# Retention, then a token and channel mixer: later channel weights, both ch1 halves ahead of ch2, and u of batch 1 turned by the crossbar

## The chip, the cores and the metric

The kernel runs on one core of a Trainium2 chip. The metric is device time in microseconds (us): the median of the runs, 207.27 us before the change. Lower is better.

## The reference

For each batch and head a state decays and collects outer products of k and v; the output of a position is q times the state, scaled. The heads' outputs, side by side, are x. Two token matmuls mix x over the sequence, and two channel matmuls mix over the channels, both with a residual.

```python
B, H, S, D = 4, 8, 768, 64          # q, k, v: [B, H, S, D] float32
gamma = 1.0 - 2.0 ** (-5.0 - arange(H)); scale = 1 / sqrt(D)
for t in range(S):
    state = gamma * state + einsum('bhd,bhe->bhde', k[:, :, t], v[:, :, t])
    y[:, :, t] = scale * einsum('bhd,bhde->bhe', q[:, :, t], state)
x  = y.transpose(0, 2, 1, 3).reshape(B, S, H * D)               # 768 x 512 per batch
h  = maximum(x.T @ w_tok1, 0) @ w_tok2                          # 768 x 256, 256 x 768
u  = x + h.T
out = u + maximum(u @ w_ch1, 0) @ w_ch2                         # 512 x 1536, 1536 x 512
```

## The kernel before

The sequence is cut into six chunks of 128 positions, the eight heads into four pairs (p = 0 to 3). The work of a batch b has two parts.

**front(b, p)**, one per pair. `load` (L256, L252) brings the rows of q, k and v of two heads, 384 KB each in float32; batch 0 uses casting transfers of the POOL queue instead (L279, L282). k is scaled on DVE (L313), q and v are cast on POOL (L292). k and q are turned so that the head's dimension lies on the partitions: by TensorE transposes (L328, L332) and a copy (L340) in batches 0 and 1, by the DMA crossbar (`crossbar`, L347, on the SP queue) from batch XK = XQ = 2 on. L361 makes the chunks' outer products, L370 and L373 run them into states on DVE, L380 and L387 put these into r16. L403 makes the scores of a half (three chunks), L416 masks them, L437 and L440 make y, L451 and L455 scale it into x, and L468 casts x on POOL. Then come the token matmuls L491, L499 (relu) and L512, the residual L519 and a cast u on POOL (L530). u is turned as well: by three L543 transposes a half and a copy L552 for batches below XU = 2, else by one crossbar transfer a pair (L566, tile u16w, two buffers).

**back(b)**, the channel mixer, in two halves of 384 positions. ch1 makes 12 tiles with 4 matmuls each (L597) and a relu (L610) into a tile h2 (two buffers); ch2 makes 3 output tiles of 12 matmuls each (L626), a residual (L635) and a store (L642). Before the change a half does ch1 and then ch2, and then the next half does the same.

**The order.** A schedule is written out by the program itself. Every step is an `Op` with an engine, a priority, an occupation, a latency, what it depends on, and the buffers that it takes (`Slot`, counts in BUFS). `arrange` lists the Ops by a planned time: it keeps one free time for each engine and one for each transfer ring (SP and POOL), lets two rings share, and picks the next Op by priority among those that can start. The order it finds is what each engine issues; each engine works through its own list strictly in turn, so a step whose input is late holds up all that stand behind it on its engine. Before batch 0's mixer starts, L194 fills PE's planned gaps with matmuls on zeros.

**Weights.** `weight` issues wt1, wt2, two pieces of the ch1 weights (512 and 1024 KB in float16) and the ch2 weights (1536 KB) on the POOL queue with a cast (L203). All rows of batch 1 wait for the second ch1 piece; the wait is added by hand:

```python
if b == 1:
    tc.add_manual_dep(dma.ins, wops["c1", 1].ins.ins.name, ...,
                      reason="the weights come first")
```

The ch2 weights stand right behind it on the same queue, with no wait of their own.

Of the kernel before, what the change touches and what calls it, by code (L numbers as in the profile page):

```python
# [17 lines left out]
def kernel(  # L18
# [11 lines left out]
    nc = tc.nc  # L30
    B, H, S, D = q.shape
    P = 128
# [62 lines left out]
                x=3, uT=3, h2=2, o=3, r16=NR, fa=5, ba=3)  # L95
    SEM, GUARD = 80, 100
    EARLY, LATE, DIRECT = 1000, 12, 3
    LONG, XK, XQ, XU, XBAR = 2, 2, 2, 2, 1500
    RING = dict(SP=3, POOL=8)
    QLONG = 1200  # L100
    ASIDE, RACT = ((1, 1), (1, 3), (2, 1), (2, 3), (3, 1), (3, 3)), ()
    KPOOL = ()
    FILL, TOKBA = 0.75, 2
    ops = []

    class Slot:
# [15 lines left out]
    def arrange():  # L122


        way = {}
        for op in reversed(ops):
            if op.first is not None:
                way[op] = way.get(op, 0) + op.lat + SEM
                for d in op.deps:
                    way[d] = max(way.get(d, 0), way[op])  # L130
        for op in ops:
            if op.first is not None:
                op.prio = (op.prio[0], 0, EARLY * op.first - way[op], op.first)
        free = dict(PE=5700, ACT=5000, DVE=4600, POOL=1100, SP=1300, SPring=1300, POOLring=1300)
        taken = {t: [] for t in BUFS}
        todo, order, ring = list(ops), [], dict(SP=[], POOL=[])
        while todo:
            best = []
            for op in todo:
                if any(d.end is None for d in op.deps):  # L140
                    continue
                start = free[op.eng]
                if op.dma and len(ring[op.eng]) >= RING[op.eng]:
                    start = max(start, ring[op.eng][-RING[op.eng]])
                for d in op.deps:
                    if d.eng == op.eng and (d.dma or d.eng == "PE"):
                        continue
                    start = max(start, d.end + (30 if d.eng == op.eng else SEM) + op.guard)
                more = {}
                for s in op.takes:  # L150
                    q = taken[s.tag]
                    n = len(q) + more.get(s.tag, 0) - BUFS[s.tag]
                    more[s.tag] = more.get(s.tag, 0) + 1
                    if n >= 0:
                        old = q[n]
                        if any(u.end is None for u in old.users):
                            break
                        start = max([start] + [u.end + SEM for u in old.users])
                else:
                    best.append((start, op))  # L160
            t = min(b[0] for b in best)

            eng = min(best, key=lambda b: (b[0], b[1].prio))[1].eng
            start, op = min((b for b in best if b[1].eng == eng and b[0] <= t + 20),
                            key=lambda b: b[1].prio)
            free[op.eng] = start + op.occ
            op.start = start
            if op.dma:

                mine, other = op.eng + "ring", ("POOL" if op.eng == "SP" else "SP") + "ring"  # L170
                at = max(free[mine], start + (op.occ + 200 if op.eng == "POOL" else 50))
                both = max(0, free[other] - at)
                shared = min(op.dma, both // 2)
                free[mine] = at + op.dma + shared
                free[other] += shared
                op.end = free[mine] + 1600
                ring[op.eng].append(free[mine])
            else:
                op.end = start + op.lat
            for s in op.takes:  # L180
                taken[s.tag].append(s)
            todo.remove(op)
            order.append(op)
        return order
# [14 lines left out]
    wops = {}  # L199

    def weight(key, ns, out, src):
        def emit():
            return nc.gpsimd.dma_start(out=out, in_=src.rearrange("(i p) j -> p i j", p=P))  # L203
        wops[key] = Op("POOL", (0,) if key[0] != "c2" else (2, 0, 0), 800, 800, emit, dma=ns)

    weight(("t1", 0), 2000, wt1, moe_w_tok1)
# [3 lines left out]
    weight(("c2", 0), 7800, wc2, moe_w_ch2)  # L210


    queue, sp_done = [], [None]
    x_add, uT_done, y_done, t1_done, t2_done = {}, {}, {}, {}, {}
    xs, uTs = {}, {}
    rcount = [0]
# [1 line left out]
    def front(b, p):  # L218
        first = b == 0
# [23 lines left out]
        def load(nm):  # L243
            src, slot = srcs[nm]

            def emit():
                t = tile_of(slot, sb, [P, 2 * NC, D], FP)
                rows = src[b, 2 * p:2 * p + 2]
                eng = nc.gpsimd if first and p else nc.sync
                if nm == "q" and b < LONG:  # L250

                    dma = eng.dma_start(  # L252
                        out=t.rearrange("p (h f i) d -> p h f (i d)", h=2, f=2),
                        in_=rows.rearrange("h (f p i) d -> p h f (i d)", f=2, p=P))
                else:
                    dma = eng.dma_start(out=t, in_=rows.rearrange("h (c p) d -> p (h c) d", p=P))  # L256
                if b == 1:
                    tc.add_manual_dep(
                        dma.ins, wops["c1", 1].ins.ins.name,
                        mybir.DependencyInfo(mybir.DependencyClass.Sync, mybir.DependencyReason.DATA),  # L260
                        reason="the weights come first")
                return dma
            ns = QLONG if nm == "q" and b < LONG else 1750
            if first and p:
                o = Op("POOL", (0,), 1000, 1000, emit, [], [slot], dma=ns)
                queue.append(o)
            else:
                o = Op("SP", (0, b, p), 100, 100, emit,
                       deps=[sp_done[-1]] + ([wops["c1", 1]] if b == 1 else []), takes=[slot], dma=ns)
                sp_done.append(o)  # L270
            return o

        def cast(slot, nm):
# [24 lines left out]
        if first and p == 1:  # L298
            queue.append(Op("POOL", (0,), 520, 520, lambda: nc.gpsimd.affine_select(
                out=mask, in_=mask, compare_op=ALU.is_ge, fill=0.0,  # L300
# [43 lines left out]
        def crossbar(src, dst, dep):  # L344
            def emit():
                d = tile_of(dst, sb, [P, S], F16)
                return nc.sync.dma_start_transpose(  # L347
                    out=d.rearrange("d (c t) -> d c t", t=P),
                    in_=src.tile.rearrange("p c h d -> p (c h d)" if src is K else "p c d -> p (c d)"))
            return Op("SP", (-1, b, p), 100, 100, emit, [dep], [dst], [src], dma=XBAR)  # L350
        kt = crossbar(K, KT, kc) if b >= XK else turn(K, KT, kc, "DVE" if first else "ACT")
        qt = crossbar(Q, QT, qc) if b >= XQ else turn(Q, QT, qc, "ACT")

# [73 lines left out]
        for hf in range(2):  # L427
# [41 lines left out]
            tk = [X] if p == 0 and hf == 0 else []  # L469
# [31 lines left out]
        tt, uc = [], None  # L501
        wide = b >= XU
        T, UW = Slot(FA), Slot("u16w")
        for hf in range(2):
# [27 lines left out]
            uc = op("POOL", 450, 510, emit, [ad, uc] if wide else [ad], [U16] if new else [], [X] if new else [X, U16])  # L532
# [14 lines left out]
            if first or hf == 1:  # L547
                def emit(hf=hf, T=T):
                    if UT.tile is None:
# [3 lines left out]
                tk = [UT] if (b, "uT") not in uT_done else []  # L553
                dep = [] if tk else [uT_done[b, "uT"]]
                e = op("ACT", 380 if first else 700, 480 if first else 800, emit, [tt[-1]] + dep, tk,
                       [T] if tk else [T, UT])
# [5 lines left out]
        if wide:  # L562
            def emit():
                if UT.tile is None:
                    tile_of(UT, sb, [P, NP, S], F16)
                return nc.sync.dma_start_transpose(  # L566
                    out=UT.tile[:, p].rearrange("d (c t) -> d c t", t=P),
                    in_=UW.tile.rearrange("p c d -> p (c d)"))
            tk = [UT] if (b, "uT") not in uT_done else []
            e = Op("SP", (-1, b, p), 100, 100, emit, [uc] + ([] if tk else [uT_done[b, "uT"]]), tk,  # L570
                   [UW] if tk else [UW, UT], dma=XBAR)
            if tk:
                uT_done[b, "uT"] = e
            for s in range(2):
                uT_done[b, p, s] = e
# [3 lines left out]
    def back(b):  # L579
# [3 lines left out]
        def op(eng, occ, lat, emit, deps=(), takes=(), uses=()):  # L583
            seq[0] += 1
            return Op(eng, ((1 if eng == "PE" else 0), b, seq[0]), occ, lat, emit, deps, takes, uses)
        for sh in range(2):
            H2 = Slot("h2")
            rel = []
            for ft in range(NF):
# [17 lines left out]
                def emit(ft=ft, A=A, H2=H2):  # L607
                    if ft == 0:
                        tile_of(H2, sb, [P, NF, SH], F16)
                    nc.scalar.activation(H2.tile[:, ft], A.tile[:, :SH], AF.Relu)  # L610
                rel.append(op("ACT", 400, 490, emit, [c1] + rel[:1], [H2] if ft == 0 else [],
                              [A] if ft == 0 else [A, H2]))
            for i in range(HC):

                parts = 2 if (b, sh, i) == (B - 1, 1, HC - 1) else 1
                CW = C // parts
                for part in range(parts):
# [25 lines left out]
                    st = op("SP", 100, 100, emit, [ad], [], [O])  # L643
                    st.prio, st.dma = (-2, b), 800 // parts


    after = {(3, "v"): (("t1", 0), ("t2", 0))}
    for p in range(NP):
# [2 lines left out]
    for b in range(1, B):  # L651
        for p in range(NP):
            front(b, p)
    for one, two in zip(queue, queue[1:]):
        two.deps.append(one)
    for b in range(B):
        back(b)
# [39 lines left out]
```

## Time and profile before

| | |
|---|---|
| runs (us) | 207.62, 207.40, 205.96, 207.27, 205.78; median 207.27 |
| profiled execution | 205.29, of which the span is 203.6 |
| granted TensorE clock | 1.0 |
| busy, share of the span | PE 95%, DVE 55%, ACT 48%, POOL 34% |
| L597 (ch1) | 384 matmuls, 68.2 us busy |
| L626 (ch2) | 300 matmuls, 68.9 us busy |
| L194 (on zeros) | 37 in the larger group, 12.0 us |
| DMA | 32.55 MB, mean 160 GB/s; q1 (SP) 25.57 MB, q0 (POOL) 6.69 MB |
| ch2 weights, issue to landing | 23.4 us |
| k rows on SP, issue to landing | median 6.4 us |

How to read it: times count from the start of the span. PE is TensorE's matmuls, PEld its weight loads, which overlap them; matmuls are pipelined, so a busy PE may hold short gaps that show only between the starts of instructions. "<-" names what an instruction waited for.

### The profile page before, as it was taken

The numbers are of one execution on the slowest core, as the hardware profiler recorded it, in microseconds if no ns is written. First come the engines' busy times: TensorE is split into PE (matmuls) and PEld (weight loads), VectorE is DVE, ScalarE is ACT, GpSimd is POOL, SyncE is SP. The second block draws the span as 40 slices with busy tenths as digits, with TensorE's granted clock in tenths as the row PEclk, the third lists the DMA queues.
The fourth block names the chain that finished last, engine by engine and source line by source line (L and its number), as shares of the span: only waits on it lengthen the run. The fifth ranks groups of instructions, "written<-read, shape, count | busy, mean of one in ns | idle before, by whom it ended". The sixth has DMA issues, their size and how long they took to land.

```text
span 203.6 us, 4737 instructions
## 1 busy us (share of the span) xinstructions
PE 194.2 (95%) x1900; PEld 119.8 (59%) x1900; DVE 111.9 (55%) x285; ACT 97.3 (48%) x211; POOL 69.4 (34%) x116
## 2 busy tenths in 40 slices
PE   7898999779999999999999999999999999999993
PEld 2554796444587766676646656566657545545552
DVE  7399863017798889897296546947682021021021
ACT  7256797651499642465404650275115604604700
POOL 7998283033155643453442144125132000000000
PEclk9999999999999999999999999999999999999999
DMA  6999999999899989998998999898531112012012
GB/s 113 175 218 186 208 210 207 245 235 262 188 272 202 187 160 234 240 215 137 202 238 185 144 228 226 157 214 125 126 92 55 39 52 103 3 52 103 0 55 103
DMA packets 88470, 32.55 MB, mean 160 GB/s; under 512 B 79328, under 2 KB 84704, under 8 KB 88448
## 3 DMA queue, kind: packets, MB, share of 16 engines
q1 hardware_dynamic: 76128, 25.57, 61.8%
q0 software_dynamic: 12320, 6.69, 23.2%
q8 instruction: 15, 0.25, 0.5%
q14 instruction: 7, 0.06, 0.1%
HBM read 26.74 MB, written 6.29 MB: 162 GB/s over the span
## 4 chain that ended last, share of the span: by engine, by line
PE 78%; DMA 13%; POOL 6%; issue 1%; DVE 1%; POOLq 0%; SPq 0%
PE ba L626 31%; PE ba L597 28%; DMA wc<-in_moe_w_ch_dram 8%; DMA kf<-in_k_dram 5%; PE fa L512 4%; PE fa L491 4%; PE fa L403 3%; PE fa L440 2%; POOL v L282 2%; PE fa L437 2%; PE fa L361 2%; POOL kf L256 2%; PE fa L332 1%; POOL q L279 1%; POOL wt L203 1%
## 5 line engine op out<-in xcount | busy, mean ns | idle before, releaser
L626 PE MATMUL ba<-wc,h 128*128 128x512 f16 (+1 forms) x300 | 68.9, 371 | 0.0
L597 PE MATMUL ba<-uT,wc 128*128 128x384 f16 x384 | 68.2, 326 | 0.0
L610 ACT ACTIVATE h<-ba 128x384 f16<-128x384 f32 x96 | 46.4, 492 | 39.2 <-PE ba L597 38.7
L597 PEld LDWEIGHTS <-wc 128*128 128x128 f16 x384 | 36.0, 98 | 22.5
L626 PEld LDWEIGHTS <-h 128*128 128x128 f16 x300 | 27.2, 98 | 25.6
L635 DVE TENSOR_TENSOR o<-x,ba 128x512 f32<-128x512 f32 (+1 forms) x25 | 16.6, 662 | 42.2 <-PE ba L626 42.1
L416 DVE TENSOR_TENSOR am<-fa,mask 128x384 f16<-128x384 f32 x58 | 29.8, 549 | 11.8 <-PE fa L403 11.7
L468 POOL CAST x<-x 128x384 f16<-128x384 f32 x30 | 15.2, 516 | 29.2 <-issue 13.8
L519 DVE TENSOR_TENSOR x<-x,fa 128x384 f32<-128x384 f32 x28 | 14.5, 550 | 11.6 <-PE fa L512 11.2
L313 DVE TENSOR_SCALAR k<-kf,gk 128x384 f16<-128x384 f32 x32 | 15.1, 512 | 7.9 <-DMA kf<-in_k_dram 7.9
L451 ACT ACTIVATE x<-fa,gy 128x192 f32<-128x192 f32 (+1 forms) x42 | 14.9, 422 | 8.6 <-PE fa L440 8.6
L373 DVE SCALAR_TENSOR_TENSOR U<-U,gp,fa 128x64 f32<-128x64 f32 x64 | 17.4, 275 | 1.1
L292 POOL CAST q<-qf 128x768 f16<-128x768 f32 x12 | 10.2, 850 | 22.4 <-DMA qf<-in_q_dram 21.2
L380 ACT ACTIVATE r<-U 64x320 f16<-64x320 f32 x16 | 7.5, 467 | 20.1 <-DVE U L373 20.1
L530 POOL CAST u16w<-x 128x384 f16<-128x384 f32 x16 | 7.9, 509 | 20.3 <-DVE x L519 20.3
L194 PE MATMUL fa<-zero 128*128 128x512 f16 x37 | 12.0, 462 | 2.2 <-DVE zero L52 1.3
L440 PE MATMUL fa<-v,am 128*128 128x64 f16 x192 | 13.6, 193 | 0.0
L440 PEld LDWEIGHTS <-am 128*128 128x128 f16 x192 | 12.1, 98 | 2.3
L491 PEld LDWEIGHTS <-wt 128*128 128x128 f16 x192 | 11.9, 98 | 2.1
L512 PEld LDWEIGHTS <-wt 128*128 128x128 f16 x192 | 11.8, 98 | 2.2
L340 ACT COPY qT<-fa 128x768 f16<-128x768 f16 x8 | 11.6, 1449 | 2.8 <-PE fa L328 2.4
L292 POOL CAST v<-vf 128x768 f16<-128x768 f32 x12 | 10.0, 830 | 6.8 <-DMA vf<-in_v_dram 6.8
(60 smaller groups left out, 176.5 us busy)
## 6 DMA issues: line engine op xcount, KB each, us to landing
out_dram<-o SPq DMA_DIRECT2D x23, 256.0 KB, 2.4
kf<-in_k_dram SPq DMA_DIRECT2D x13, 384.0 KB, 6.4
qf<-in_q_dram SPq DMA_DIRECT2D x12, 384.0 KB, 5.9
vf<-in_v_dram SPq DMA_DIRECT2D x12, 384.0 KB, 5.3
wc<-in_moe_w_ch_dram POOLq DMA_DIRECT2D x1, 1536.0 KB, 23.4
kf<-in_k_dram POOLq DMA_DIRECT2D x3, 384.0 KB, 6.7
wc<-in_moe_w_ch_dram POOLq DMA_DIRECT2D x1, 1024.0 KB, 16.0
q<-in_q_dram POOLq DMA_DIRECT2D x4, 192.0 KB, 6.1
```

The lines of the kernel that those rows point to most:

```text
L292: nc.gpsimd.tensor_copy(t, src.tile.rearrange("p (h c) d -> p h c d", h=2))
L313: (nc.gpsimd if keng == "POOL" else nc.vector).tensor_scalar(k16[:, :, j, :], src, gk[:, h:h + 1], None, ALU.mult)
L373: nc.vector.scalar_tensor_tensor(U[:, c], U[:, c - 1], gp[:, p:p + 1], o, ALU.mult, ALU.add)
L416: nc.vector.tensor_tensor(am, src[:, :HC], mask, ALU.mult)
L440: nc.tensor.matmul(o[:, j * D:(j + 1) * D], AM[2 * hf + j].tile[:, i], V.tile[:, j * NC + c], start=(c == 0), stop=(c == 0 or j == 1))
L468: nc.gpsimd.tensor_copy(X16.tile[:, half(hf)], X.tile[:, half(hf), pc])
L491: nc.tensor.matmul(acc[:, jt * P:(jt + 1) * P], wt1[:, i, jt * P:(jt + 1) * P], X16.tile[:, i], start=(i == 0), stop=(i == NC - 1))
L512: nc.tensor.matmul(acc[:, i * P:(i + 1) * P], wt2[:, jt, t], H1.tile[:, jt], start=(jt == 0), stop=(jt == NJ - 1))
L597: nc.tensor.matmul(acc[:, :SH], w[:, ct, f * P:(f + 1) * P], UT.tile[:, ct, sh * SH:(sh + 1) * SH], start=(ct == 0), stop=(ct == NP - 1))
L610: nc.scalar.activation(H2.tile[:, ft], A.tile[:, :SH], AF.Relu)
L626: nc.tensor.matmul(A.tile[:, :CW], H2.tile[:, ft, i * P:(i + 1) * P], wc2[:, ft, cs], start=(ft == 0), stop=(ft == NF - 1))
L635: nc.vector.tensor_tensor(o[:, :CW], X.tile[:, sh * HC + i, cs], A.tile[:, :CW], ALU.add)
```

## The change

Four things are changed.

1. The issue of the ch2 weights waits for the v rows of batch 1's pair 1 (PRE = 2 pairs). The dependency enters the plan, and `weight` adds it by hand to the transfer. With it the issue moves on POOL behind batch 0's last casts and the first four casts of batch 1.
2. `back` is cut into `ch1(half)` and `ch2(half)`. For batch 0 (b < TWICE = 1) both halves of ch1 come before both halves of ch2; from batch 1 on the order stays.
3. XU goes from 2 to 1: u of batch 1 is turned by the crossbar (four transfers L566 on SP) and not by 24 transposes L543 and four copies L552.
4. The planner's numbers change: a crossbar transfer occupies SP for 1220 ns (100 before) and its ring for 1200 (1500 before), and a transfer of SP that is planned after 5 us starts only when POOL's ring is free. These change the order that comes out, on every engine.

```diff
-    LONG, XK, XQ, XU, XBAR = 2, 2, 2, 2, 1500
+    LONG, XK, XQ, XU, XBAR = 2, 2, 2, 1, 1200
...
-    FILL, TOKBA = 0.75, 2
+    FILL, TOKBA, PRE, TWICE = 0.75, 2, 2, 1
...
                 both = max(0, free[other] - at)
                 shared = min(op.dma, both // 2)
+                if op.eng == "SP" and at > 5000:
+                    at, shared = max(at, free[other]), 0
...
-            return nc.gpsimd.dma_start(out=out, in_=src.rearrange("(i p) j -> p i j", p=P))
+            dma = nc.gpsimd.dma_start(out=out, in_=src.rearrange("(i p) j -> p i j", p=P))
+            for before in wops[key].deps:
+                if before.eng == "SP":
+                    tc.add_manual_dep(dma.ins, before.ins.ins.name, ...,
+                        reason="the rows come first")
+            return dma
...
-            return Op("SP", (-1, b, p), 100, 100, emit, [dep], [dst], [src], dma=XBAR)
+            return Op("SP", (-1, b, p), 1220, 1220, emit, [dep], [dst], [src], dma=XBAR)
...
-        for sh in range(2):
+        halves = {}
+        def ch1(sh):
             H2 = Slot("h2")
...
+            halves[sh] = H2, rel
+        def ch2(sh):
+            H2, rel = halves[sh]
...
+        for part in ((ch1, 0), (ch1, 1), (ch2, 0), (ch2, 1)) if b < TWICE else ((ch1, 0), (ch2, 0), (ch1, 1), (ch2, 1)):
+            part[0](part[1])
...
+    wops["c2", 0].deps.append(row_op[1, PRE - 1, "v"])
```

## The prediction

> **What bounds the kernel now.** I read the page first: slices and chain.
>
> ```profile
> PE   7898999779999999999999999999999999999993
> DMA  6999999999899989998998999898531112012012
> PE 78%; DMA 13%; POOL 6%; issue 1%; DVE 1%; POOLq 0%; SPq 0%
> ```
>
> TensorE (PE) sets the end: 78% of the chain, nearly all of it after 42 us. The DMA engines are about full in the first 27 slices (to 140 us). 13% of the chain is two transfers, and the chain in order of time (start, us, what) shows which:
>
> ```profile
> 15.16 16.02 DMA wc<-in_moe_w_ch_dram
> ...
> 31.25 9.85 DMA kf<-in_k_dram
> ...
> 41.12 0.76 DVE k L313 x2
> ...
> 41.93 0.51 PE fa L332 x6
> ```
>
> Batch 1's rows may start when the second ch1 weight piece has landed (31.2); the first tile of k then needs 9.85 us. PE's timeline shows the price:
>
> ```profile
> 34.32 5.36 PE L597 MATMUL ba<-uT,wc 128*128 128x384 f16 x32
> 41.93 0.51 PE L332 MATMUL fa<-ident,k 128*128 128x128 f16 x6 [2.25 <-DVE k L313]
> ```
>
> 48 L597 take 7.80 us in the chain's pure stretch at 169.17, 0.1625 each, so the 32 of them end their turn at 39.52 and L332 comes at 41.93: **2.41 us lost**. From 45 to 161 us PE is busy in every stretch of the table by stages, and from 161 on it runs pure L597 and L626. So the end moves by what PE's own work after 33.7 us (the first L597) gains or loses, plus any new wait.
>
> Why 9.85 us? The DMA view of three stretches (packets, MB, share), 31.5 to 34.5, 35 to 37, and 40.5 to 43.5 us:
>
> ```profile
> q0 software_dynamic: 596, 0.61, 121.9%
> ```
> ```profile
> q0 software_dynamic: 306, 0.31, 92.0%
> q1 hardware_dynamic: 300, 0.08, 29.1%
> ```
> ```profile
> q1 hardware_dynamic: 2484, 0.71, 113.7%
> ```
>
> q0 carries the ch2 weights (1536 packets of 1024 B), q1 the rows (a k or v tile is 1536 packets of 256 B). Alone, q0 moves 199 packets a us and q1 828. Together they take turns packet by packet, 153 to 150, so the rows fall to 0.04 MB a us, under a fifth of their rate. The first k tile alone in the machine, at 0.8 us, landed after 3.7 us.
>
> **The change, part by part.** Line numbers are those of before. I also read the issue order of the changed program, engine by engine.
>
> *Removed.* The 2.41 us: q1 is alone from 31.25, so k of pair 0 lands at 31.25 + 3.7 = 34.95, is scaled (0.76) by 35.8, and PE reaches L332 in the new order at 37.6. No wait. Then 24 transposes L543 of batch 1; six take 0.34 in the chain, so 4 x 0.34 = **1.36 us**. The four L552 copies (0.80 each, 3.2 on ACT) go too; ACT is 48% busy, so I count nothing. Sum: -3.77.
>
> *Added.* Four crossbar transposes of u on SP, each 1.21 us of SP and 2.9 to landing. Their u is first read by batch 1's L597, which in the new order stands behind batch 0's whole ch2 (72 L626 at 0.216 = 15.6 us), so they are covered; uncovered one would cost 4.1. Behind each on SP wait the rows of batch 2. The first scores of batch 2 run at 76.09 in the chain; their qT is issued at 70.04 and needs 3.1, so 2.9 us of slack meets two transposes (2.4) put ahead of it. Zero, with 4 x 1.21 = 4.8 less 2.9 = +1.9 as the far bound.
>
> *Moved.* Batch 0's second ch1 half goes before ch2: same matmuls, no cost. Batch 0's stores go behind the rows of batch 1 on SP; SP no longer stands at 49 to 52 us for them. The ch2 weights' issue goes on POOL from place 27 to place 45, behind the v cast of batch 1's pair 1. That cast needs the same tile, so the issue itself waits for nothing more. When is ch2 needed? PE's first L626 comes in the new order after 96 L597 and the fronts of three pairs, at about 59.
>
> *The new wait.* The weights now meet the rows of pairs 2 and 3. Two pairs' rows land one pair per 4.4 us (POOL's v casts at 44.10 and 48.52), so: k0 34.95, v0 37.5 (k to v is 4.4 less one tile of 1536/828 = 1.85), v1 41.9, k2 43.75, v2 46.3 and k3 48.2 if alone. The v1 cast ends at 42.9 (0.83), the weights' issue takes 1.04, and the first POOL load's packets (issue 1.42, 0.92 long) began 1.0 after that: q0 starts at 44.9. Then v2 lacks (46.3 - 44.9) x 828 = 1160 packets, and k3 all its 1536. The 1536 weight packets at 153 a us take 10.0 us, to 54.9; rows pass 1500 meanwhile. So v2 lands at about 52.6 and k3, with 1200 left at 828, at **56.3**. Adding bytes gives the same: 48.2 + 1536/199 = 55.9.
>
> Who waits? On DVE, in the new order, the scaling L313 of k3 stands ahead of four state steps L373 of pair 2, the scaling L455 of pair 1 and then the masks, sums and state of pair 2. DVE's durations are in its timeline (start, us):
>
> ```profile
> 61.25 0.54 DVE L455 TENSOR_TENSOR x<-fa,gyw 128x384 f32<-128x384 f32 x1
> 61.72 0.90 DVE L373 SCALAR_TENSOR_TENSOR U<-U,gp,fa 128x64 f32<-128x64 f32 x3
> ...
> 65.57 0.75 DVE L313 TENSOR_SCALAR k<-kf,gk 128x384 f16<-128x384 f32 x2
> ```
>
> From 56.4: 0.75 + 4 x 0.30 + 0.54 = 58.9, POOL's cast L468 (516 ns) and two hand-overs of 0.1 end at 59.6: pair 1's token matmul L491 may start. PE would reach it after 88 L597 (14.3), 45 transposes (2.5), 30 L361 (0.84), 30 L403 (1.1), two whole y groups (1.26) and 24 of L491 and L512 (1.34): 33.66 + 21.3 = 55.0, or 55.5 with 0.1 for each group of small matmuls between wide ones. So 4.1 late. Next on DVE stand two masks, two L519 and one L387, 2.4 us to 61.3, and the second score group of pair 2 (L403), due on PE at 56.8, follows: **4.5 late**. Most of it is PE standing, first for v2 (due 50.5, cast by 53.5), then for k3. Bounds: if q0 starts 2 us later, k3 is mostly through and lands by 53.3, wait 1.6; if v2's delay adds the POOL casts behind it, 7. I take 4.5, nearest the packet rows.
>
> Sum: -3.77 + 4.5 = **+0.7 us**. The profiled execution took 205.29 (span 203.6, 1.7 outside); that becomes 206.0. Its time is 2.0 below the median of the runs, 207.27; I add the same 0.7 there: 208.0.
>
> A rule to weigh. The Trainium skill (DMA: Bandwidth & Descriptors, "SWDGE vs HWDGE vs iDMA") has an engine switch queues only at the end of a packet of preferably up to 4096 B. That would be four weight pieces against sixteen row pieces, equal bytes: v2's rest and k3, 0.69 MB, would be through after 0.69 MB of weights, near 52, with a wait of about 0.5, and the sum would be -3.3 (204.0). The case's 306 to 300 says piece by piece at any size, so I go by the row.
>
> **Rivals.** *No wait worth naming* (the weights' first packets come after k3, or the rows get a bigger share): -3.77, **203.5**. For it: every other supply in the new order is ahead of PE's need. Against: 150 a us, and that PE reaches k3's transposes at 55.0, where it was 61.4 before, while the same bytes must still pass.
>
> *v2 blocks POOL* (the slower side). Place: POOL, where v2's cast stands ahead of the second x cast of pair 0 and of all u casts. If v2 lands later than 54, its cast ends at 55 or more, pair 0's token matmul (due 50.7) starts 5 late, and SP stands at the first u transpose with batch 2's rows behind it, so k3's chain comes on top: wait 7, **210.5**. For it: one more half us of weights ahead of v2 costs v2 several; against: 52.6 by the sum.
>
> *The crossbar crowds SP* while the rows behind the weights do well: -3.77 + 1 (half of that wait left) + 1.9 = **206.4**.
>
> **How the numbers follow.** Forecast 0.44 (its own range 206.0 to 209.6), no wait 0.26, POOL blocked 0.22, crossbar 0.08. A measurement here tells about 1%, 205.2 to 209.3, from no change. Faster 0.26 (no wait); same 0.38 of the forecast + 0.08 = 0.46; slower 0.06 + 0.22 = 0.28. The range takes most of both ends: 203.4 to 210.8.
>
> **What would show it.** Right: no idle PE before L332 of pair 0; 96 L597 of batch 0 ahead of the first L626; a k tile of batch 1 with some 8 to 11 us to landing in the stretch 45 to 57; DVE idle before an L313 for DMA kf, and PE idle 3 to 6 us in sum between 50 and 63; packets of q0 and q1 in equal counts there. Wrong: k3 landed by 51, or PE without a gap. The crossbar's case would show as PE waiting for qT of batch 2 between 70 and 90.

## The result, and the profile after

The changed kernel takes 208.13 us (median; 204.19 to 213.52), the kernel before beside it 207.18; the ratio is **0.9974 [0.9951, 0.9998]** for the like runs: 0.3% faster, where 0.3% slower was forecast. The ratio leaves out runs more than 1.5% above their kernel's fastest, which are 27 of the 46 of the changed kernel, so by the plain medians it is 0.95 us slower. The profiled execution of after took 206.9 us, its span 205.2 (before 205.29 and 203.6).

Line numbers of after, as far as used: L343 is before's L332 (turn of k or q), L324 its L313 (scaling of k), L384 its L373 (state step), L414 its L403 (scores), L610 its L597 (ch1), L643 its L626 (ch2). In an experiment they move by a few lines. A landing is given here when the profile releases the engines that wait for it; the expectations below give some up to 0.8 us earlier, at the tile's last pieces. The page of after, slices and chain, then PE's timeline around the old and the new place:

```profile
PE   7598999999599999999999999999999999999993
PEclk9999999999969999999999999999999999999999
PE 78%; DMA 8%; DVE 7%; ACT 2%; issue 1%; POOL 1%; POOLq 0%; DVEq 0%
```
```profile
36.73 0.98 PE L610 MATMUL ba<-uT,wc 128*128 128x384 f16 x5
37.55 0.50 PE L343 MATMUL fa<-ident,k 128*128 128x128 f16 x6
...
53.68 0.23 PE L414 MATMUL fa<-qT,kT 64*128 64x128 f16 x1
56.64 0.34 PE L414 MATMUL fa<-qT,kT 64*128 64x128 f16 x5 [2.73 <-DVE U L384]
```

The old wait is gone: the turn of k of pair 0 follows the ch1 matmuls without idle time. A new one stands at 54 to 57, in the first group of scores of pair 2 (the 5 in slice 11 of PE), and in the next slice PEclk shows a 6. The chain has the transfer (start, us, what), and VectorE's timeline names the cause (in the brackets: idle before, and what ended it):

```profile
43.06 11.61 DMA kf<-in_k_dram
```
```profile
54.69 0.75 DVE L324 TENSOR_SCALAR k<-kf,gk 128x384 f16<-128x384 f32 x2 [3.38 <-DMA kf<-in_k_dram]
55.36 1.22 DVE L384 SCALAR_TENSOR_TENSOR U<-U,gp,fa 128x64 f32<-128x64 f32 x4
```

DVE stands 3.38 us for k of pair 3, which lands at 54.67; the state steps behind it keep the PSUM tile (`fa`) that PE's scores need next. Why k is late is in the DMA view, at 49 to 51 and at 53 to 55 us (packets, MB, share):

```profile
q0 software_dynamic: 315, 0.32, 95.9%
q1 hardware_dynamic: 285, 0.07, 26.4%
```
```profile
q0 software_dynamic: 269, 0.28, 80.7%
q1 hardware_dynamic: 266, 0.18, 38.1%
```

The two queues again move their pieces in equal counts. (In the second stretch 222 of q1's 266 pieces are the 768 B pieces of the next q rows, hence its MB.) And the windows view, around the slice with the 6 (PE, PEld, DVE, ACT and POOL busy, then the granted clock, DMA share and GB/s):

```profile
57.00:58.00 1.00, 1.00 (x10) 0.67 (x10) 1.00 (x3) 0.47 (x2) 0.51 (x1) 0.77 1.19 209
58.00:59.00 1.00, 1.00 (x10) 0.83 (x9) 0.56 (x2) 0.11 (x1) 0.51 (x1) 0.50 1.25 260
59.00:60.00 1.00, 1.00 (x10) 0.83 (x9) 0.80 (x2) 0.23 (x1) 0.18 (x1) 0.50 1.28 273
60.00:61.00 1.00, 1.00 (x13) 1.00 (x12) 0.23 (x1) 0.96 (x2) 1.00 (x2) 0.53 1.10 184
```

From 57.53, just behind the wait, TensorE was granted half its clock for 3.41 us, though it was busy: half of that, **1.7 us**, is lost. The prediction has no such term.

### The profile page after: what moved, and what is told of

It is laid out like the page before. It is cut to its first block, busy times and chain, and to the rows that moved or that the text cites. A ratio compares the mean times of both kernels' runs of the same rounds, so it can differ in the third digit from the quotient of the medians.

```text
span 205.2 us, 4691 instructions
## 1 busy us (share of the span) xinstructions
PE 193.9 (94%) x1876; PEld 118.8 (58%) x1876; DVE 114.3 (56%) x285; ACT 94.9 (46%) x207; POOL 69.3 (34%) x116
## 4 chain that ended last, share of the span: by engine, by line
PE 78%; DMA 8%; DVE 7%; ACT 2%; issue 1%; POOL 1%; POOLq 0%; DVEq 0%
PE ba L643 31%; PE ba L610 27%; DMA kf<-in_k_dram 6%; PE fa L502 5%; PE fa L523 4%; PE fa L414 3%; DMA v<-in_v_dram 3%; DVE k L324 2%; PE fa L451 2%; DVE am L427 2%; DVE U L384 2%; PE fa L448 2%; PE fa L372 2%; ACT qT L351 1%; PE fa L343 1%
## 5 line engine op out<-in xcount | busy, mean ns | idle before, releaser
L610 PE MATMUL ba<-uT,wc 128*128 128x384 f16 x384 | 70.3, 328 | 0.0
L643 PE MATMUL ba<-wc,h 128*128 128x512 f16 (+1 forms) x300 | 68.0, 371 | 0.0
L610 PEld LDWEIGHTS <-wc 128*128 128x128 f16 x384 | 35.7, 98 | 21.4
L643 PEld LDWEIGHTS <-h 128*128 128x128 f16 x300 | 27.4, 98 | 26.4
L541 POOL CAST u16w<-x 128x384 f16<-128x384 f32 x24 | 11.9, 507 | 37.8 <-DVE x L530 37.6
L324 DVE TENSOR_SCALAR k<-kf,gk 128x384 f16<-128x384 f32 x32 | 16.6, 560 | 7.2 <-DMA kf<-in_k_dram 7.1
L384 DVE SCALAR_TENSOR_TENSOR U<-U,gp,fa 128x64 f32<-128x64 f32 x64 | 17.6, 276 | 1.2
L502 PEld LDWEIGHTS <-wt 128*128 128x128 f16 x192 | 12.3, 101 | 2.0 <-issue 0.2
L197 PE MATMUL fa<-zero 128*128 128x512 f16 x37 | 11.2, 440 | 2.4 <-DVE zero L52 1.3
L414 PE MATMUL fa<-qT,kT 64*128 64x128 f16 x192 | 10.1, 219 | 3.4 <-DVE U L384 2.7
L523 PEld LDWEIGHTS <-wt 128*128 128x128 f16 x192 | 12.0, 99 | 2.2 <-issue 0.3
L523 PE MATMUL fa<-h,wt 128*128 128x128 f16 x168 | 12.6, 223 | 0.0
```

The source lines that it names most:

```text
L324: (nc.gpsimd if keng == "POOL" else nc.vector).tensor_scalar(k16[:, :, j, :], src, gk[:, h:h + 1], None, ALU.mult)
L384: nc.vector.scalar_tensor_tensor(U[:, c], U[:, c - 1], gp[:, p:p + 1], o, ALU.mult, ALU.add)
L414: nc.tensor.matmul(a[j][:, i], KT.tile[r, t], QT.tile[r, t], start=True, stop=True)
L502: nc.tensor.matmul(acc[:, jt * P:(jt + 1) * P], wt1[:, i, jt * P:(jt + 1) * P], X16.tile[:, i], start=(i == 0), stop=(i == NC - 1))
L523: nc.tensor.matmul(acc[:, i * P:(i + 1) * P], wt2[:, jt, t], H1.tile[:, jt], start=(jt == 0), stop=(jt == NJ - 1))
L610: nc.tensor.matmul(acc[:, :SH], w[:, ct, f * P:(f + 1) * P], UT.tile[:, ct, sh * SH:(sh + 1) * SH], start=(ct == 0), stop=(ct == NP - 1))
```

## The experiments

The theory: the new wait is k of pair 3 standing behind the ch2 weights' packets, and each wait of PE costs a half clock of 3.41 us or more behind it. Rivals: the crossbar, the mixer's order, a fixed order of instructions. (No run takes back the mixer's order or the planner's numbers by themselves, so what each of them is worth is not shown.) "Clock 0.99" below is a run's mean granted clock; one stretch of 3.41 us at half in 205 is 0.992.

**One row block of the ch2 weights.** Only the first of twelve is transferred; the rest is set to zero, so that the output is another.

```diff
+            if key[0] == "c2":
+                dma = nc.gpsimd.dma_start(out=out[:, :1], in_=src[:P].rearrange(...))
...
+            if (b, p) == (1, 0):
+                nc.vector.memset(wc2[:, 1:], 0.0)
```

> The changed kernel with only the first of 12 row blocks of the ch2 weights transferred (128 packets for 1536); the other eleven blocks of the tile are set to zero by DVE once, behind the scaling of batch 1's first k tile, where DVE stands idle from 36 to 40.8 us. So ch2 is wrong in value and the same in instructions. Theory (the packets of the weights take turns with v2 and k3): v2 lands near 47.2 and k3 near 49, DVE's wait for kf near 51 goes to under 0.3 us, PE has no gap over 0.5 us after 37 us, the clock stays 1.0, and the span is 205.2 - 2.8 - 1.7 - 0.3 = 200.4 (200.0 to 201.2). Rival (the gap comes from DVE's order or the five score buffers, not from the transfer): the gap near 53.7 keeps 1.5 us or more and the span stays above 203.

Measured: 202.26 us, ratio 0.9798 [0.974, 0.9856], clock 1.0 in all four runs. k of pair 3 landed at 51.58, just as DVE came free, and DVE's timeline has no wait ahead of its scaling (there L327):

```profile
51.29 0.23 DVE L386 COPY U<-fa 128x64 f32<-128x64 f32 x1
51.61 0.75 DVE L327 TENSOR_SCALAR k<-kf,gk 128x384 f16<-128x384 f32 x2
```

The order of the engines is that of the changed kernel, mixer and crossbar included (the filling with zeros on DVE apart), so the weights' bytes are the cause of the new wait and of what follows it. This run also measures, with most of the weights' transfer gone, what was removed by itself: its last matmul starts at 197.03, before's at 200.07, so 3.04 us.

**The weights early again.** All else as changed; the ch2 weights are issued straight behind the second ch1 piece.

```diff
+            if key == ("c1", 1):
+                nc.gpsimd.dma_start(out=wc2, in_=moe_w_ch2.rearrange("(i p) j -> p i j", p=P))
```

> The changed kernel with the ch2 weights' transfer issued straight behind the second ch1 piece, as before the change; every other instruction keeps its place on every engine. Theory (the 9.85 us of the first k tile were the weights' packets): the first k tile of batch 1 lands near 41.1 again, PE stands at the first k turn from 37.6 to 41.9 (4.3 us) and q's turn adds a little, no wait for k3 near 54; the wait of 4.3 is 1.5 more than the 2.8 it replaces, and the clock may fall to half after it (1.7). Span 204.5 without the fall, 206.5 with it. Rival (the weights never held the rows back; the order did it): first k tile lands by 36, span 201 to 202.

Measured: 208.92 us, ratio 1.0116 [1.0045, 1.0187]. The wait is back at the first turn of k: k of pair 0 landed at 41.59 (35.36 as changed), PE stood 5.11 us, and 6.83 us at half clock began within that wait. There was no wait at pair 3. So the weights' place decides which rows are late.

**The weights behind k of pair 3.**

```diff
+                if (b, p, nm) == (1, 2, "v"):
+                    dma = nc.gpsimd.dma_start(out=wc2, in_=moe_w_ch2.rearrange(...))
+                    tc.add_manual_dep(dma.ins, row_op[1, 3, "k"].ins.ins.name, ...)
```

> The changed kernel with the ch2 weights issued behind POOL's cast of v2 and behind the landing of k3, so behind three pairs' rows and a k tile and not two pairs'; all other instructions keep their places. Theory (bytes only change places): v2 lands near 47 and k3 near 49, no wait at 53.7; the weights start near 51.5 and land 10 to 11 us later, 62 to 63, while PE reaches the first ch2 matmul at 59.2, so PE stands there 3 to 4.5 us instead, the clock falls after it, and the span is 204.5 to 207. Rival (the place of the weights is free once k3 is through): no wait over 1 us, span 200.5 to 202.

Measured: 210.18 us, ratio 1.02 [1.0137, 1.0263]. k of pair 3 landed at 50.40, but the wait moved twice: POOL stood 1.03 us at the issue with an x cast behind it (PE idle 1.85), and the weights landed at 65.58, after PE wanted them (idle 2.89). Two half-clock stretches of 3.41 us followed. Two waits of together 4.7 us cost more than the one they replaced.

**Matmuls of zeros in the new wait** (12 ahead of the scores that wait), and, in the kernel *before*, 10 ahead of its first turn of k:

```diff
+            a.fill = 12 if (b, p, hf) == (1, 2, 0) else 0
...
+            if getattr(o, "fill", 0):
+                idle[0] = o.fill
```
```diff
+            t.fill = 10 if (b, p) == (1, 0) and src is K else 0
```

> The changed kernel with 12 matmuls on zeros (0.216 us each, 2.6 us) put on PE ahead of the first score group of batch 1's pair 2, where PE stood from 53.7 to 56.6 us. They write the score tile that the group takes, and run inside the wait. Theory (the wait of 2.8 us for k3 stays, and the clock at half for 3.4 us after it comes from PE standing still): the same DVE wait for kf near 51 to 54.7, PE without a gap over 0.5 us there, granted clock 1.0 from 55 to 65 and a span of 203.2 to 203.8 where the changed kernel had 205.2 (it loses 1.7 less). Rival (the half clock has another cause, or PE's load brings it): the clock still falls to 0.5 after 57 us, the span stays 205 or more, and 12 matmuls may cost up to 0.3.

> The kernel before with 10 matmuls on zeros (2.2 us) put on PE ahead of the k turn of batch 1's pair 0, where PE stands from 39.5 to 41.9 us; they write the tile that the turn takes. Nothing else is changed. Theory (PE's standing still brings a stretch of 3.4 us at half clock in many executions, 1.7 us, and not in others): granted clock 1.0 throughout, and the median falls from 207.2 to 205.3, a ratio near 0.992. Rival (the half clock has another cause): no change, ratio 0.998 to 1.003.

Measured: the first, 208.81 us, ratio 0.9981 [0.9934, 1.0029], is inconclusive on time. In its profile k of pair 3 landed at 59.35 and PE still stood 4.81 us after the zeros; half of its runs had clock 1.0 (205.15 to 207.14). The second is clear: 205.61 us, ratio **0.995 [0.9917, 0.9983]**, clock 0.997 or more in all 12 runs. PE's timeline there:

```profile
39.52 2.32 PE L194 MATMUL fa<-zero 128*128 128x512 f16 x10
41.80 0.51 PE L332 MATMUL fa<-ident,k 128*128 128x128 f16 x6
```

The wait is as long as it was, and the median is 1.5 us lower than that of before beside it (207.12). Of 81 runs of before beside these experiments, 24 had clock 0.997 or more (median 205.40), 56 had 0.992 (207.25) and one 0.983. So idle time of 2.25 us brings on the half clock in most executions of before, at 1.85 us each, and the profiled one, at clock 1.0 throughout, was one of the others.

**u of batch 1 by matmul again.**

```diff
-    LONG, XK, XQ, XU, XBAR = 2, 2, 2, 1, 1200
+    LONG, XK, XQ, XU, XBAR = 2, 2, 2, 2, 1200
```

> The changed kernel with u of batch 1 turned by TensorE again (XU = 2): 24 transposes and four copies back, four crossbar transfers gone. Theory (the crossbar part is worth its PE time and nothing else): the plan is 1.37 us longer, the wait for k3 stays 2.5 to 3.2, span 1.2 to 1.6 longer at the same clock, 206.6 with one stretch at half clock. Rival (the crossbar crowds SP and costs as much as it gives): span equal or shorter, and the rows of batch 2 land 2 us earlier or more.

Measured: 208.11 us, ratio 1.0057 [1.0008, 1.0107], against 0.9974 for the whole change: the crossbar part is worth 0.8% (1.7 us; the intervals allow 0.2 to 3.2). That is rough, as its profile has one more half-clock stretch, at 10.84, ahead of any change. Its wait at pair 3 was 2.24 us, below the forecast. Its last matmul starts 2.07 us after that of after (203.49 against 201.42); 1.17 of this stood already at the first ch1 matmul (34.81 against 33.64), and the wait is 0.49 shorter. That leaves 1.39, which is the 1.36 that was counted for the 24 transposes.

**Smaller pieces for the weights.**

```diff
+                    out=out.rearrange("p i (g j) -> p i g j", g=4),
+                    in_=src.rearrange("(i p) (g j) -> p i g j", p=P, g=4))
```

> The changed kernel with the ch2 weights' transfer cut into pieces of 128 elements (256 B in SBUF, 6144 packets) and not 512 (1024 B, 1536 packets); same bytes, same place, same order on all engines. Theory (the two queues take turns packet by packet whatever the size): with equal packets the rows get half the bytes and not a fifth; together some 400 packets a us each; k3 lands near 52 to 52.5 and not 54.4, PE's gap near 53.7 falls from 2.8 to about 1, the clock stays 1.0, the weights land at about 60 as before, span 201.7 to 203. Rival (turns go by bytes, or the weights' queue is served first): k3 at 54 or later, gap 2.5 or more, span 205; or POOL needs so long for four times the pieces that its casts are late.

Measured: 211.58 us. The pieces stayed at 1024 B in the trace, so this was the changed kernel over again, and piece size was not tried. Its profile shows another execution of it: k of pair 3 landed at 58.76, PE stood 7.15 us, half clock 10.24 us.

**Later due times** for k and v of pairs 2 and 3 and the weights in the planner, so that DVE's scaling of k stands behind the state steps:

```diff
-                op.end = free[mine] + 1600
+                op.end = free[mine] + 1600 + getattr(op, "late", 0)
...
+    wops["c2", 0].late, row_op[1, 3, "k"].late, row_op[1, 2, "v"].late = 3700, 4400, 400
```

> The changed kernel with three due times of its planner set to what the profile of the changed kernel shows: k3 of batch 1 is planned 4.4 us later, v2 0.4 and the ch2 weights 3.7. No transfer is changed; the lists of the engines are (the planner puts the work that needs k3 behind other work). Theory (the wait of 2.8 us comes from k3's late landing meeting a list that expects it early, and the half clock from that wait): k3 lands at 54 to 55 as before, DVE and PE have no gap over 1 us near it, the clock stays 1.0; the plan itself is 1.2 us longer, so the span is 205.2 - 2.8 - 1.7 + 1.2 = 201.9 (201.5 to 203). Rival (what is saved at k3 is spent at the ch2 weights, which land near 60): a gap of 2 us or more before the first ch2 matmul, span 204 or more.

Measured: 206.67 us, ratio 0.9984 [0.994, 1.0028]. In the profile k landed at 59.99, and now the turn of k of pair 3 itself waited (idle 2.80 up to 60.82, half clock 6.83 us). Another place, the same cause.

**The weights in two halves.**

```diff
+            c = 6 if key[0] == "c2" else None
+            out_, src_ = (out[:, :c], src[:c * P]) if c else (out, src)
...
+                if (b, p, nm) == (1, 2, "v"):
+                    nc.gpsimd.dma_start(out=wc2[:, 6:], in_=moe_w_ch2[6 * P:].rearrange(...))
```

> The changed kernel with the ch2 weights in two transfers: the first six of twelve row blocks where the change puts all of them (packets from about 47), the other six issued by POOL straight behind its cast of v of pair 2 of batch 1 (issue about 50, packets from about 53). Theory (the new wait is k of pair 3 of batch 1 standing behind the weights' packets, and the half clock follows from that wait): only 768 packets of 1024 B stand against the rows, so k of pair 3 lands about half way between the 50.9 us of the run with one block and the 54.4 us of the changed kernel, near 52.5; DVE waits about 1.2 us, PE under 1 us, no half-clock stretch behind it; the weights land as before near 60 to 61, ahead of the first ch2 matmul. Time about 203.5, ratio about 0.983. Rival (whatever the order, the half clock and the wait come from the mixer order or the crossbar, not from the weights): 208, ratio 0.997, with a wait of 2.5 us or more at the same matmul. Second rival (the same bytes in the same stretch, only cut in two: k of pair 3 lands at 54 to 55 as before because the second half takes up the queue again): 207 to 208.

Measured: 206.73 us, ratio 1.0006 [0.9968, 1.0044], not what the theory said. DVE's wait is about that of the changed kernel, PE stood 2.57 us, and 3.41 us at half clock followed:

```profile
54.96 0.64 DVE L329 TENSOR_SCALAR k<-kf,gk 128x384 f16<-128x384 f32 x1 [3.22 <-DMA kf<-in_k_dram]
```

The DMA view at 48 to 51 says why: the counts were not equal here.

```profile
q0 software_dynamic: 550, 0.56, 114.3%
q1 hardware_dynamic: 143, 0.04, 7.5%
```

The rows got a fifth of the pieces in these three microseconds, and k of pair 3 landed at 54.93, after the first half (53.91). The second half's pieces started only at 53.54, a microsecond before the tile's last.

**Halves and due times together, without and with ten matmuls of zeros, and the changed kernel again.** The edits are the last two; the zeros stand ahead of the turn of k of pair 3.

> Both earlier moves together: the ch2 weights in two transfers of six row blocks (as in the run with the halves), and later due times for k and v of the last two pairs in the planner, so that VectorE's scaling of k of pair 3 stands behind the state step, the masks and the x scaling that it held up. In the run with the halves alone k of pair 3 landed at 54.2; in the run with the due times alone the PE work that needs nothing of pair 3 reached to 57.7. Theory (the new wait is k of pair 3 of batch 1 alone, and a half-clock stretch of 3.41 us stands behind a wait of over 2 us only): no PE gap over 0.5 us between 50 and 60, granted clock 1.0 in most runs, the run with the halves at clock 1.0 (205.0) less its wait of 2.6 us, plus about 1.2 us for the other order: 203.6; ratio about 0.985. Rival (what the weights take from the rows comes back later in any order, at the queries of pair 3 or at the first ch2 matmul): a gap of 2 to 3 us there, 206 to 207, ratio 0.997.

> The same with ten matmuls of zeros ahead of the turn of k of pair 3 of batch 1. Theory: where k of pair 3 has landed in time they are pure cost, ten times about 0.11 us: 1.1 us more than the run without, 204.7. Rival (k of pair 3 lands late in many executions, and the half clock follows): they keep TensorE awake, the clock stays at 1.0 in nearly all runs, and the median is below that of the run without them.

> The changed kernel once more, unedited, beside the two others. Theory: the size of the new wait is set by when the rows get a turn beside the ch2 weights, and that differs between executions; so the landing of k of pair 3, the PE gap behind it and the granted clock differ from the first profile (54.4 us, 2.8 us, one stretch of 3.41 us), while what lies ahead of 47 us does not by more than 0.8 us. Time 206 to 208, ratio 0.995 to 1.0. Rival (the wait is fixed by the order of instructions): the same landing and the same gap within 0.5 us.

Measured: without zeros 204.83 us, ratio 0.9922 [0.988, 0.9964]; with them 205.05 us, ratio **0.9897 [0.9866, 0.9928]**; the changed kernel again 209.13 us (205.51 to 213.25, 6 runs; no ratio). k of pair 3 landed at 54.40 and 54.64 and found no PE waiting for it. Without zeros PE stood 1.55 us for v of pair 3, up to 62.32, and 3.41 us at half clock followed from 62.61; 4 of 12 runs have a clock of 0.992 or less. With zeros 9 of 10 runs had a full clock, and the page reads:

```profile
PE   7598999999999999999999999999999999999993
PEclk9999999999999999999999999999999999999999
PE 85%; DVE 6%; DMA 3%; ACT 2%; issue 1%; POOL 1%; POOLq 0%; DVEq 0%
```

Between the start and the last slice none is under 9, of PE or of its clock, and DMA's share of the chain is 3% where it was 8. Whether the zeros help further is not decided (the two intervals overlap). The repeat of the changed kernel had the same instructions in the same order, and this page and timeline:

```profile
PE   7598999999379999999999999999999999999993
PEclk9999999999958999999999999999999999999999
```
```profile
58.27 0.50 PE L414 MATMUL fa<-qT,kT 64*128 64x128 f16 x5 [4.36 <-DVE U L384]
```

k of pair 3 came at 56.30, PE stood 4.36 us instead of 2.73, and the half clock lasted 6.83 us instead of 3.41. So the wait has no fixed size: in the three profiles of this kernel, the one meant to have smaller pieces among them, PE stood 2.73, 4.36 and 7.15 us.

## Why the prediction was wrong, step by step

*Removed, -3.77: the mechanism right, the size too large.* k of pair 0 landed at 35.36 (34.95 forecast), its turn ran at 37.55 (37.6) with no idle time. The run with one row block gives 3.04 us for all that was removed. The 1.36 for the transposes is borne out by the run that takes them back (1.39); where the other 0.7 stayed isn't known. One reading of the first k tile was too simple: equal turns do not fill its 9.85 us, for the prediction's own first stretch (31.5 to 34.5) has no packet of q1. The tile's first packet came 3.55 us after its issue, where the changed kernel's came after 1.05.

*Added, the crossbar at nothing: held.* PE waits for nothing that the view of waits lists between 62 and 110 us, where the crossbar's rival wanted a wait for qT.

*v blocks POOL (rival, 210.5): did not come.* v of pair 2 landed at 49.24, not after 54, and POOL cast it at 49.29.

*The new wait, +4.5: the term that was mis-sized.* The mechanism was right: counts of 315 to 285, DVE standing at the scaling of k of pair 3, and PE behind it. Equal bytes, worked out from the packet size that the Trainium skill gives (DMA: Bandwidth & Descriptors, "SWDGE vs HWDGE vs iDMA"), would have given the rows four times the pieces; the row held. But the packets of q0 began at about 47, not 44.9: the weights' issue stood at 44.06, not 42.9, and packets came 3 us behind its start, where 2 were assumed. So k landed at 54.67, not 56.3, the weights at 60.38, not 54.9 (still ahead of the first L643 at 64.03, which has the 96 L610 ahead of it as forecast), and PE's idle time was 2.73 us. The place on PE was another too: the first scores of pair 2, reached at 53.91, came free by the state step that released their PSUM tile, 1.97 us behind k's landing, and not by the chain through the x scaling and the token matmul that the sum walked along. With k at 56.3 these would have made a wait of 4.4, so it is the landing that was mis-sized. The bounds of 1.6 and 7 hold this and the repeat's 4.36, not the 7.15 of the run meant to have smaller pieces; the point lay too high for the profiled execution.

*The clock: the term that was missing.* A half clock of 3.41 us behind the new wait cost 1.7. The sum for the profiled executions is then -3.04 + 2.73 + 1.7 = +1.4; the last matmul moved from 200.07 to 201.42, +1.35. It closes. That the forecast for this execution, +0.7, lies near is luck: 0.7 too much was taken off, 1.8 too much was put on, and 1.7 was left out.

*The step to the median: the one that turned the sign.* "I add the same 0.7 there" held the 2.0 us between before's profiled execution and its median to be no part of the change. The matmuls of zeros in before show that it is: 56 of 81 runs of before have a half-clock stretch, and where zeros fill the very wait that the change takes away no run has one. For such runs the change removes 3.04 + 1.85 and adds 2.73 + 1.7, so -0.5 us, 0.2%: the measured 0.9974 is -0.5. Medians at like clock say somewhat less, 0.3 us: 205.40 before and 205.12 after (5 runs) at 0.997 and more; 207.25 and 207.00 (18 runs) with one stretch.

*The spread: not in the prediction.* The other 23 of the 46 runs after have a clock of 0.984 or less, with medians of 210.88 (13 runs) and 212.87 (10 runs, at 0.976 or less); before has one such run of 81. The two profiles of the same kernel at 0.982 and 0.974 show a longer wait, 4.36 and 7.15 us, with 6.83 and 10.24 us at half clock. So, as far as these profiles tell, half of the executions lose more at the new place than nearly every run of before lost at the old one. That the plain median, 208.13, lies at the forecast 208.0 is luck as well.

The change as a whole moved a wait from one row tile to another, kept the half clock that goes with it, and made its size less certain; in the like runs it is a gain only by the crossbar part (ratio 1.0057 without it).

## What to carry to other kernels

A large background load did not get cheaper here by being moved past some rows: it made the next tile in line late, and the engine that scales that tile held back everything queued behind it. Moving the waiting instruction and splitting the load are worth trying together; here neither alone helped, and both gave 0.8% over the kernel before (1% with the zeros). When a wait of TensorE of some 2 us is removed or made, price the half clock behind it too, and look at the clocks of all runs before taking a profiled execution as typical.

## What the runs showed of the hardware

*The half clock comes in units.* Every stretch ahead of the last matmul was a multiple of 3.41 us and began 1.8 to 4.2 us after PE fell idle, so often with PE busy again: one behind idle time of 1.55 us (4 of 12 runs of that kernel have such a clock), 1.85, 2.24, 2.25 (most runs of before, by their clock), 2.57, 2.73 and 2.89; two (6.83) behind 4.36, 4.81 and 5.11, in one profile behind 2.80; three (10.24) behind 7.15. None followed the 2.25 of before's profile, nor an early 2.09 in the run with the later due times; one began at 10.84 in the run with u turned by matmul, 3.5 us after PE fell idle for 1.31. The Trainium skill (TensorE: Matmul & The Clock Gate, "What's actually happening") tells of a free-running window of 3413 ns, which agrees. The same page ("Why this matters for your kernels") asks for no idle time above about 3 us; here less was enough, and the measurement decides.

*A queue that joins can hold the other down.* Equal counts were the rule once both queues ran (whether a turn is one piece or several doesn't show), but in the first microseconds the rows' share of the pieces differed from run to run, down to a fifth, and k of pair 3 landed between 54.67 and 59.35 in the changed kernel, its repeats and the run with zeros, which all issue the same transfers in the same order. In the three profiles with the latest landings (58.76, 59.35, and 59.99 with the later due times) the rows stopped altogether for a microsecond behind v of pair 2, with k issued long before; the DMA view of the run meant to have smaller pieces lists the weights' queue alone at 48.3 to 49.3:

```profile
q0 software_dynamic: 159, 0.16, 114.8%
```

What decides it wasn't found.
